# Eight matmuls without a reader, placed in TensorE's stream behind the first part of the last V and ahead of the last group's total, in a two-block decode attention kernel

## The chip, the core and the metric

The kernel runs on one core of one Trainium2 chip. The metric is the device time of one execution in microseconds. The times shown are medians of several executions. Beside them stands one execution that was recorded by the hardware profiler; its span runs from the first to the last instruction, and its own time is a little longer than its span. Engines are called by the profile's names: PE is TensorE's matmul side and PEld its weight loads, DVE is VectorE, ACT is ScalarE, POOL is GpSimd, SP is SyncE, which issues nearly all DMAs.

## The reference

Two independent blocks A and B, of the same shapes, decode one token each with 32 heads of 128 elements over 8192 cached positions. Everything is bf16 in HBM.

```python
q = (x @ wq).reshape(B, Sq, H, Dh).transpose(0, 2, 1, 3)     # x: 1 x 1 x 512, wq: 512 x 4096
scores = einsum("bhqd,bhkd->bhqk", q, k_cache) * Dh ** -0.5  # k_cache: 1 x 32 x 8192 x 128
p = softmax(scores, axis=-1)
o = einsum("bhqk,bhkd->bhqd", p, v_cache)                    # v_cache: 1 x 32 x 8192 x 128
y = o.transpose(0, 2, 1, 3).reshape(B, Sq, H * Dh) @ wo      # wo: 4096 x 512
out = concatenate([y_A, y_B], axis=-1)                       # 1 x 1 x 1024
```

K and V of one block are 64 MiB each, so some 285 MB are read for 2 KB of output.

## The kernel before

**Tiling.** The 64 heads go in 16 rounds of G = 4 heads; rounds 0 to 7 are block A, 8 to 15 block B. In a round a head has 32 partitions and each partition 256 positions (T), so one K or V of a round is a tile of 128 partitions by 256 x 128 elements, 8 MiB. `kn` holds two K tiles, `vn` holds one V tile. At the end `kn` also receives the output weights `wo` of both blocks, in the room of K tiles that are done with.

**One round r.** DVE multiplies K in place by q, in two halves (L280). PE then sums over the 128 elements of a head with matmuls against an identity: `scores` (L425 to L438) runs four tiles, alternately in the two halves of the PSUM tensor `rps`, each with one small matmul that opens the bank (L430) and a loop of four turns with four matmuls of 512 columns each (L432 to L436). DVE reduces each tile to 64 scores per partition (L308). After the fourth tile come the maximum (L313, PE's transpose L476, L315, PE's broadcast L478), ACT's four exponentials into `pt` (L383) and the row sums, which PE adds up over the partitions (L484). Then PE waits for V (L485, semaphore s_v) and multiplies: 64 matmuls of 512 columns into `acc` (L492), which go in turn to four groups of 32 PSUM partitions. The last of them raises c_pv. DVE picks the useful blocks of `acc` in the next round (`part`, L283 to L292), and PE adds them up over the partitions (`total_of_group`, L440 to L442).

**The DMA queue.** SP issues everything in a fixed order: K of round n+2 when the scores of round n are through, V of round n+1 when c_pv says that the V matmuls of round n are done with `vn`. The V of rounds 14 and 15 comes in two DMAs, positions 0 to 191 and 192 to 255 (VT = 192, L207 and L208), on two semaphores. So in these two rounds PE does 48 of the 64 matmuls, enters an `If` and waits for the second part (`w_v2`, L489 and L490), and does the other 16.

**The end.** In round 14 SP also issues `wo` of A (L229) and the first 16 heads of `wo` of B (L230, `load_wob(0)`), then the two parts of the last V when c_pv of round 14 has come (L231), and six smaller pieces of `wo` of B (L233): three of 4 heads, then 2, 1 and 1. In round 15, between the scores and its V, PE runs `mid` (L447 to L467): it lays out the outputs of earlier heads and does the 48 output matmuls of A's 32 and B's first 16 heads (L461). Behind the loop over rounds, PE does the other 16 heads of B piece by piece as the pieces land (L497 to L509, the matmuls at L506, two per head). Ahead of the piece with g = 2 it does `total_of_group` for the last group (L500), which waits for DVE's `part` (c_st). The piece of 2 heads begins with the last group's heads, so it also waits for DVE's normalised output of that group (L297, c_o, waited for at L503). Two copies (L352, L386) and one DMA (L389) end the kernel.

**Order.** The order on each engine is written out by hand, engine by engine; engines meet only at the semaphores named above.

## Time and profile before

| | |
|---|---|
| median of 3 runs | 666.0 us |
| lowest, highest | 665.41, 666.83 us |
| the profiled execution's own time | 665.7 us |
| its span | 664.2 us |
| mean granted clock of TensorE | 0.784 |
| PE, DVE, ACT busy | 385.1 us (58%), 363.3 us (55%), 76.0 us (11%) |
| read from HBM | 285.21 MB, 429 GB/s over the span |

Lines beginning with L are lines of the kernel before. In rows of the timeline the first number is the start in us from the beginning of the span, the second the time from the first start to the last end of the instructions in the row, "x16" their number, and the bracket the idle time of the engine ahead of them with what ended it. "PEclk" is the clock that TensorE was granted, as a share of full speed. The ends of matmuls are modelled by the profiler.

### The profile page before, as it was taken

The numbers are of one execution on the slowest core, as the hardware profiler recorded it, in microseconds if no ns is written. First come the engines' busy times: TensorE is split into PE (matmuls) and PEld (weight loads), VectorE is DVE, ScalarE is ACT, GpSimd is POOL, SyncE is SP. The second block draws the span as 40 slices with busy tenths as digits, with TensorE's granted clock in tenths as the row PEclk, the third lists the DMA queues.
The fourth block names the chain that finished last, engine by engine and source line by source line (L and its number), as shares of the span: only waits on it lengthen the run. The fifth ranks groups of instructions, "written<-read, shape, count | busy, mean of one in ns | idle before, by whom it ended". The sixth has DMA issues, their size and how long they took to land.

```text
span 664.2 us, 7946 instructions
## 1 busy us (share of the span) xinstructions
PE 385.1 (58%) x2398; PEld 169.4 (25%) x2398; DVE 363.3 (55%) x250; ACT 76.0 (11%) x211; POOL 2.3 (0%) x12
## 2 busy tenths in 40 slices
PE   1719392854819275481928548192854819285776
PEld 0203141322304132230413223041322304132332
DVE  1046757548292654829275482927547292754821
ACT  1710202020010202001020200102020010202020
POOL 1000000000000000000000000000000000000000
PEclk9968787786958778695877869597786959778789
DMA  9999999999999999999989999999999999989998
GB/s 379 442 442 442 442 442 391 430 442 442 442 442 399 422 442 442 442 442 442 442 387 434 442 442 442 442 442 414 406 442 442 442 442 442 434 387 458 426 413 344
DMA packets 6472, 285.22 MB, mean 429 GB/s; under 512 B 708, under 2 KB 1224, under 8 KB 1608
## 3 DMA queue, kind: packets, MB, share of 16 engines
q1 hardware_dynamic: 6464, 285.22, 99.5%
q10 hardware_dynamic: 8, 0.00, 0.0%
HBM read 285.21 MB, written 0.00 MB: 429 GB/s over the span
## 4 chain that ended last, share of the span: by engine, by line
DMA 82%; PE 15%; issue 1%; ACT 1%; SPq 0%; ACTq 0%; DVE 0%
DMA vn<-in_A_v_cache_dram 41%; DMA vn<-in_B_v_cache_dram 34%; PE acc L492 13%; DMA kn<-in_B_wo_dram 5%; PE yps L419 2%; DMA vn<-in_A_wq_dram 2%; ACT qmem L372 1%; SPq L220 0%; PE yps L506 0%; SPq L208 0%; ACTq L43 0%; ACTq L372 0%; DVE out_sb L352 0%
## 5 line engine op out<-in xcount | busy, mean ns | idle before, releaser
L280 DVE TENSOR_TENSOR kn<-kn,qmem 128x16384 bf16<-128x16384 bf16 x32 | 276.7, 8688 | 49.6 <-DMA kn<-in_A_k_cache_dram 37.1
L436 PE MATMUL rps<-kn,ident 128*128 x1024 | 236.2, 383 | 0.4
L492 PE MATMUL acc<-vn,pt 128*32 128x512 bf16 x1024 | 92.0, 537 | 153.5 <-DMA vn<-in_A_v_cache_dram 80.4
L308 DVE TENSOR_REDUCE s_sb<-rps 128x64 f32<-128x512 f32 x64 | 44.3, 692 | 166.8 <-PE rps L436 166.8
L436 PEld LDWEIGHTS rps<-kn,ident 128*128 128x128 bf16 x1024 | 96.5, 98 | 110.4 <-issue 22.3
L492 PEld LDWEIGHTS acc<-vn,pt 128*32 128x32 bf16 x1024 | 38.4, 129 | 200.6 <-issue 194.3
L378 ACT ACTIVATE negb<-bmp 128x4 f32<-128x4 f32 x16 | 2.8, 173 | 547.3 <-PE bmp L478 547.3
L383 ACT ACTIVATE pt<-s_sb,negb 32x256 bf16<-32x256 f32 x64 | 54.9, 858 | 4.3 <-ACT negb L378 3.0
L484 PE MATMUL misc<-rsum,ones_f 128*128 128x4 f32 x32 | 9.2, 358 | 56.4 <-ACT pt L383 56.4
L285 DVE TENSOR_SCALAR om<-acc,msk 128x128 f32<-128x128 f32 x16 | 5.6, 350 | 41.8 <-PE acc L492 41.8
L484 PEld LDWEIGHTS misc<-rsum,ones_f 128*128 128x128 f32 x32 | 7.8, 304 | 58.2 <-ACT pt L383 57.7
L419 PE MATMUL yps<-vn,xT 128*128 x64 | 17.4, 422 | 8.5 <-ACT qmem L372 4.4
L288 DVE SCALAR_TENSOR_TENSOR om<-acc,msk,om 128x128 f32<-128x128 f32 x48 | 16.8, 351 | 5.9
L430 PE MATMUL rps<-ones_bf,zrow 1*128 1x1 bf16 x64 | 11.0, 172 | 15.6 <-DVE kn L280 15.4
L476 PE MATMUL mtp<-ident_f,m 128*1 128x128 f32 x32 | 6.1, 270 | 22.6 <-DVE m L313 22.6
L372 ACT CAST qmem<-yps 32x128 f32 x64 | 16.4, 256 | 9.4 <-PE yps L419 8.6
L430 PEld LDWEIGHTS rps<-ones_bf,zrow 1*128 1x128 bf16 x64 | 5.8, 91 | 42.8 <-issue 42.8
L383 ACT ACTIVATION_READ_ACCUMULATOR pt<-s_sb,negb 32x1 f32 x64 | 15.9, 248 | 0.0
L419 PEld LDWEIGHTS yps<-vn,xT 128*128 x64 | 6.6, 103 | 18.9 <-issue 16.0
L478 PE MATMUL bmp<-gm,ones_f 1*128 1x4 f32 x32 | 6.1, 258 | 7.3 <-DVE gm L315 7.3
L297 DVE TENSOR_TENSOR oD<-mtp,rinv 128x4 f32 x15 | 2.4, 162 | 13.6 <-PE mtp L442 13.6
L315 DVE TENSOR_REDUCE gm<-mtp 1x4 f32<-1x128 f32 x16 | 4.5, 279 | 8.9 <-PE mtp L476 8.9
(56 smaller groups left out, 50.9 us busy)
## 6 DMA issues: line engine op xcount, KB each, us to landing
vn<-in_B_v_cache_dram SPq DMA_DIRECT2D x2, 6144.0 KB, 28.0
vn<-in_A_wq_dram SPq DMA_DIRECT2D x1, 4096.0 KB, 12.2
vn<-in_B_wq_dram SPq DMA_DIRECT2D x1, 4096.0 KB, 21.4
vn<-in_B_v_cache_dram SPq DMA_DIRECT2D x2, 2048.0 KB, 32.5
kn<-in_A_wo_dram SPq DMA_DIRECT2D x1, 4096.0 KB, 27.8
kn<-in_B_wo_dram SPq DMA_DIRECT2D x1, 2048.0 KB, 32.3
kn<-in_B_wo_dram SPq DMA_DIRECT2D x3, 512.0 KB, 34.1
kn<-in_B_wo_dram SPq DMA_DIRECT2D x1, 256.0 KB, 35.2
```

Source lines behind the costliest of these rows:

```text
L280: e.tensor_tensor(k, k, qflat[:, bass.ds(q, Dh)].unsqueeze(1).broadcast_to([P, HM, Dh]), ALU.mult).then_inc(c_mul, 2)
L288: e.scalar_tensor_tensor(om[t % 2][:], acc[:, t * Dh:(t + 1) * Dh], msk[:, t:t + 1], om[(t + 1) % 2][:], ALU.mult, ALU.add).then_inc(*((c_ ...
L308: e.tensor_reduce(s_sb[:, h * HT:(h + 1) * HT], rps[:, h % 2, :].rearrange("p (t d) -> p t d", d=DW), AX.X, ALU.add).then_inc(c_sr, 1)
L372: i = e.copy(qflat[p, bass.ds(r * (2 * Dh) + j * Dh, Dh)], yps[j][p, h * Dh:(h + 1) * Dh])
L383: e.activation(pt[p, 0:T, h], s_sb[p, :], AF.Exp, bias=negb[p, h:h + 1], scale=scale, accum_out=rsum[p, h:h + 1]).then_inc(c_p, 4)
L419: i = e.matmul(yps[j][:], xT[:, bass.ds(x0 + c, 1)].broadcast_to([P, P]), vn[:, bass.ds(w0 + (c * H * Dh + j * G * Dh), G * Dh)], start=(c ...
L430: e.matmul(rps[:, tile, 0:1], zrow[:], ones_bf[0:1, 0:1], start=True, stop=False, skip_group_check=True)
L436: m = e.matmul(ro, ident[:], src, start=False, stop=False, skip_group_check=True)
L476: e.matmul(mtp[0:1, 0:P], m1[:], ident_f[:], start=True, stop=True).then_inc(c_gx, 1)
L478: e.matmul(bmp[:, 0:G], ones_f[0:1, :], gm[:], start=True, stop=True).then_inc(c_bc, 1)
L484: e.matmul(misc[:, 0:G], ones_f[:], rsum[:], start=True, stop=True)
L492: m = e.matmul(acc[k:k + HP, :], ptf[:, g * W * G:g * W * G + HP], vn[:, g * W * Dh:(g + 1) * W * Dh], start=(g < G), stop=(g >= NG - G))
```

## The change

A helper `turn_over(n)` is added to PE's stream. It runs n times a loop body of one matmul: the identity as weights, the first 512 columns of `vn` as the moving operand, the first half of `rps` as the target. Each of them starts and stops its own accumulation. Nothing reads the result: in rounds 14 and 15 the scores of the round have been reduced by then, and the next tile of scores opens the bank anew. It waits for no semaphore and raises none.

It is called at two places: with n = 5 inside the `If` for the last two rounds, ahead of `w_v2()`, so in round 14 and in round 15; and with n = 3 behind the loop over rounds, ahead of the last `total_of_group()`. The text holds eight matmuls by this count; one execution runs 5 + 5 + 3 = 13. The instructions of the other engines, and the order of all others on PE, are the same as before.

```diff
+                def turn_over(n):
+
+                    with e.Fori(0, n):
+                        e.matmul(rps[:, 0, :], ident[:], vn[:, 0:512], start=True, stop=True)
+
                 with e.Fori(0, N) as r:
...
                     for g in range(NG):
                         if g * W == VT:
                             with e.If(r >= N - 2):
+                                turn_over(5)
                                 w_v2()
...
                 for g in range(1, len(WOB)):
                     h0, n, rows = WOB[g]
                     if g == 2:
+                        turn_over(3)
                         total_of_group()
```

## The prediction

> **What bounds the kernel now.** I read the page first: the rows of DMA, then the chain that ended last.

> ```profile
> DMA  9999999999999999999989999999999999989998
> GB/s 379 442 442 442 442 442 391 430 442 442 442 442 399 422 442 442 442 442 442 442 387 434 442 442 442 442 442 414 406 442 442 442 442 442 434 387 458 426 413 344
> ...
> DMA 82%; PE 15%; issue 1%; ACT 1%; SPq 0%; ACTq 0%; DVE 0%
> ```

> The 16 DMA engines are busy in all 40 slices, at 442 GB/s in most, and 82% of the chain is DMA. The kernel is bound by reading its caches. PE's 15% stand in the chain because each V is issued when PE's last matmul of the V before has freed `vn`; whether such a piece costs time depends on whether the queue runs dry meanwhile. So next I followed the chain through the last two rounds.

> ```profile
> 618.13 5.96 PE acc L492 x64
> ...
> 626.38 35.17 DMA kn<-in_B_wo_dram
> ...
> 661.59 0.64 PE yps L506 x6
> ...
> 662.28 0.29 PE yps L506 x2
> ...
> 662.59 0.41 DVE out_sb L352
> ```

> The end is set by landings. Piece g = 4 of `wo` lands at 626.38 + 35.17 = 661.55, the last piece at about 662.24, since its two matmuls start at 662.28. Behind that are 0.29 us of PE, 0.41 us of DVE and the output's DMA up to 664.2. The queue at that time, from the timeline of SP and the lists of DMA issues (the number behind KB is the time from issue to landing):

> ```profile
> 605.18 0.43 SPq L220 DMA_DIRECT2D kn<-in_B_wo_dram  x1
> 624.11 0.80 SPq L208 DMA_DIRECT2D vn<-in_B_v_cache_dram  x2
> 624.96 14.94 SPq L220 DMA_DIRECT2D kn<-in_B_wo_dram  x6
> ```

> ```profile
> kn<-in_B_wo_dram SPq DMA_DIRECT2D x1, 2048.0 KB, 32.3
> ```

> ```profile
> vn<-in_B_v_cache_dram SPq DMA_DIRECT2D x1, 6144.0 KB, 27.9
> vn<-in_B_v_cache_dram SPq DMA_DIRECT2D x1, 2048.0 KB, 32.5
> ```

> When the last V is issued at 624.11, the queue still holds work up to 605.18 + 32.3 = 637.5: a reserve of 13.4 us. And the six small pieces, which at 0.43 us each would take under 3 us to issue, take SP 14.94 us, up to 639.90: SP itself is held back by a queue that is full. The last V's parts land at 624.11 + 27.9 = 652.0 and, issued 0.4 us later, near 657.0.

> PE's end, and the two rows of DVE that it exchanges with:

> ```profile
> 652.17 2.77 PE L492 MATMUL acc<-vn,pt 128*32 128x512 bf16 x48
> 657.06 1.05 PE L492 MATMUL acc<-vn,pt 128*32 128x512 bf16 x16 [2.12 <-DMA vn<-in_B_v_cache_dram]
> 658.27 0.60 PE L506 MATMUL yps<-kn,o 128*2 128x256 bf16 x8 [0.16 <-DMA kn<-in_B_wo_dram]
> 659.99 0.38 PE L442 MATMUL mtp<-selh,om 128*128 128x4 f32 x2 [1.12 <-DVE om L288]
> 660.30 1.14 PE L506 MATMUL yps<-kn,o 128*2 128x256 bf16 x16
> 661.59 0.96 PE L506 MATMUL yps<-kn,o 128*2 128x256 bf16 x8 [0.15 <-DMA kn<-in_B_wo_dram]
> ```

> ```profile
> 658.16 0.35 DVE L285 TENSOR_SCALAR om<-acc,msk 128x128 f32<-128x128 f32 x1 [6.95 <-PE acc L492]
> ...
> 660.48 0.17 DVE L297 TENSOR_TENSOR o<-mtp,rinv 128x4 bf16<-128x4 f32 x1 [0.46 <-PE mtp L442]
> ```

> Here are the two waits: 2.12 us ahead of the last 16 matmuls of V and 1.12 us ahead of the total. The last group's output is ready at 660.48 + 0.17 = 660.65, the piece that uses it lands at 661.55: PE's chain has 0.90 us to spare behind the first wait.

> **The change part by part.** Thirteen matmuls are added; nothing is removed. First their price, which no row shows directly. The nearest rows are loops and V matmuls at both clocks:

> ```profile
> 618.51 0.18 PEld L492 LDWEIGHTS acc<-vn,pt 128*32 128x32 bf16 x4 [0.24 <-issue]
> ...
> 622.35 0.18 PEld L492 LDWEIGHTS acc<-vn,pt 128*32 128x32 bf16 x4 [0.24 <-issue]
> ...
> 622.99 0.58 PEld L492 LDWEIGHTS acc<-vn,pt 128*32 128x32 bf16 x16 [0.46 <-issue]
> ...
> 624.11 3.76 PE L436 MATMUL rps<-kn,ident 128*128 x16
> ...
> 636.06 3.73 PE L436 MATMUL rps<-kn,ident 128*128 x16
> ```

> ```profile
> 12.96 0.89 issue
> 13.85 5.11 PE yps L419 x12
> ```

> A row of L436 is the same kind of matmul as the added one (identity, 512 columns, all four row and column groups), with four turns of a loop in it: 3.76 / 16 = 0.235 us each at the full clock. V's matmuls run four side by side: 48 in 2.77 us is 4 x 2.77 / 48 = 0.231 us for one stream of 512 columns at the full clock. The rows from 618.51 to 622.35 are ten groups of four, so a group of four costs (622.35 - 618.51) / 9 = 0.427 us at half clock. The four turns of L436 thus cost at most 3.76 - 16 x 0.231 = 0.06 us beyond the matmuls. Entering a loop costs between nothing and the 0.89 us from the landing of wq to the first matmul of the first loop on PE; I take 0.2, nearer to the low end, because PE has its instructions in hand here and waits for no semaphore. Five matmuls: 5 x 0.235 + 0.2 = **1.4 us**, bounds 5 x 0.231 = 1.2 and, at half clock with the slow entry, 5 x 0.427 + 0.89 = 3.0. Three: 3 x 0.235 + 0.2 = **0.9 us**, bounds 0.7 and 2.2. Nothing below zero is among them, as a matmul gives no time back except through the clock, which is a rival below.

> [...]

> *Round 14, five.* There is no wait to fill here. The weight loads of the last 16 matmuls begin at 622.99, 0.46 us of weight-load idle behind the group before, and the 64 matmuls stand in the chain as one unbroken piece from 618.13. So 1.4 us is pure addition. It delays c_pv, and with it the issue of the last V and the six pieces, from 624.11 to 625.5. The queue's reserve of 13.4 us covers this; without that cover it would cost the 1.4 us in full. The pieces' issue still ends with the full queue, at 639.90. DMA cost: **0**. It also delays all of round 15's scores by 1.4 us, since their tiles follow each other on PE; the fourth then ends near 641.2.

> *From there to the last V* there is the softmax chain and `mid`, and here the clock speaks. The table by windows, cut where the clock steps:

> ```profile
> 639.76:643.17 3.41, 1.10 (x7) 0.67 (x6) 1.58 (x5) 0.45 (x2) 0.00 (x0) 1.00 1.07 461
> 643.17:646.59 3.42, 2.53 (x18) 0.99 (x22) 1.74 (x10) 3.17 (x8) 0.00 (x0) 0.50 1.06 460
> 646.59:650.00 3.41, 3.41 (x36) 1.11 (x32) 0.00 (x0) 0.00 (x0) 0.00 (x0) 0.50 1.07 461
> 650.00:653.41 3.41, 2.61 (x38) 1.14 (x34) 0.69 (x1) 0.00 (x0) 0.00 (x0) 1.00 0.72 308
> 653.41:656.83 3.42, 1.53 (x31) 0.60 (x20) 0.00 (x0) 0.00 (x0) 0.00 (x0) 1.00 0.91 382
> 656.83:660.24 3.41, 1.90 (x26) 0.90 (x26) 1.49 (x5) 0.00 (x0) 0.00 (x0) 1.00 1.01 401
> ```

> The columns are the window, its length, the busy time of PE, PEld, DVE, ACT and POOL, PEclk, the DMA share and GB/s. The steps fall on a grid of 3.41 us. A window with 1.10 us of PE is followed by half clock, one with 1.53 us is not; a full one is followed by full clock, one with 2.53 us is not. On the same grid the change brings 1.4 us more of scores into the first of these windows and pushes 0.8 us of the softmax's matmuls out: 1.7 us, above 1.53, so `mid` runs at full clock. Its 48 matmuls of four side by side took

> ```profile
> 645.47 4.98 PE L461 MATMUL yps<-kn,o 128*2 128x512 bf16 x48
> ```

> and would take 48 x 0.231 / 4 = 2.8: 2.2 us back against the 1.4 lost. Then PE waits for the first part of V at 652.0 and begins its 48 as before. On another position of the grid, with `mid` as slow as before, the 1.4 us arrive whole: the 48 begin at 653.6.

> *Round 15, five.* The 48 end at 654.9, or at 656.3 in the bad case; with 1.4 us more, 656.3 or 657.7. The second part lands at 657.0: cost **0**, or 0.7 us, which the 0.90 us to spare behind it take up. If the fillers were dearer, what is late next is the last group's output.

> *The three.* They start behind the eight matmuls at 658.27 + 0.60 = 658.9 and end at 659.8, ahead of the total at 659.99: cost **0**. At their upper bound they would end at 661.1 and the total would be 1.1 late, 0.2 past the spare.

> SBUF and PSUM: the fillers read `vn` while DMA writes `kn` and `vn`, as the scores and V's matmuls do all along; slices of 442 GB/s stand over busy and idle PE alike, so I count nothing, in either direction. The sum is 0 + 0 + 0 against the profiled execution: 665.7 us, its span 664.2 and 1.5 around it. It lies 0.3 under the median of 666.0. I put the forecast at **665.8**, between the two, since the profiled execution had no half clock in its end and a slower run may have.

> **The rivals.** A measurement of this kernel can tell about 0.2%, 1.3 us, from no change.

> *Slower: PE becomes the bound at the end.* The mechanism is the delay of round 14 carried through round 15 and added to the five there. Cover is 2.12 us of wait and 0.90 us behind it, 3.0 in all; the forecast's demand in the bad case is 1.4 + 1.4 = 2.8. From 1.5 us for five matmuls on, the end moves, by twice what lies above that. For: the margin is thin, and entry is a guess. With the slow entry at full clock five cost 5 x 0.235 + 0.89 = 2.1: 4.2 - 3.0 = 1.2 late, 667.0. At half clock throughout, 6.0 - 3.0 = 3.0, 668.8. Against: `mid` runs nearly unbroken for 5 us, which brings the clock back, and the clock may return more than is lost.

> *Faster: the clock in the end.* The two waits are where a window could fall under 1.53 us of PE. Then the last 16 of V cost 16 x 0.427 / 4 = 1.7 instead of 1.05, and the 24 small ones behind the total up to double their pace; with the landing times fixed that makes some 0.5 to 1.4 us. The fillers add 1.2 and 0.7 us of PE to these windows and forbid it. For: the spread of the three runs, 665.41 to 666.83, is of that size, and the grid need not lie the same in each run. Against: the table above shows PEclk 1.00 from 650.00 on, so there is nothing to gain in it, and what stands behind the last landing at full clock is not shortened. Gone from a slow run: 666.8 - 1.4 = 665.4, still within 0.2% of 666.0.

> [...]

> *The change doesn't do what it says:* that the fillers miss the waits is true for five of the thirteen, as worked out; 666.0 as well, by the reserve.

> **How the numbers follow.** No difference, in any of its forms: 0.86 (forecast 0.66, clock regained in part of the runs 0.14, rule or missed waits 0.06). Slower by PE: 0.10 over 1.3 us; its milder form, up to 667.0, is inside "same". Faster by over 1.3 us needs less than 664.7, 0.7 under the lowest run, and would need landings that come earlier: 0.04. The range goes from 665.1, somewhat under the lowest run, to 667.1, the slow entry at full clock.

> **What would show it.** Right: the chain again ends in the small pieces of `wo`, landing within 0.3 us of 661.55 and 662.24; SP's issue at 625.3 to 625.7 and ending near 640; the five in 1.2 to 1.7 us; a wait left ahead of the last 16 of V, or under 0.9 us of delay. Wrong: L506's last matmuls released by DVE's output instead of a landing; fillers at over 0.4 us each; a queue that is empty after 637.

## The result, and the profile after

| | before | after |
|---|---|---|
| median of 7 runs each | 666.1 us | 668.71 us |
| lowest, highest | 665.41, 666.83 us | 666.41, 669.14 us |
| ratio of after to before | | 1.0037, 95% interval 1.0027 to 1.0047 |
| the profiled execution's own time | 665.7 us | 669.1 us |
| its span | 664.2 us | 664.0 us |
| its time outside the span | 1.5 us | 5.1 us |
| instructions in PE's built program | 478 | 492 |

The change makes the kernel slower by 0.37%, and yet the span did not get longer. All seven executions of the changed kernel have spans of 663.9 to 664.1 us. What grew is the part of an execution that lies outside the span: 4.3 to 5.1 us in six of them and 2.3 in the seventh. Ahead of the span the profiles show no growth: the first packet of instructions is recorded 11.1 us ahead of the first instruction before, and 11.2 after. Of the kernel before, 68 more executions were taken beside the experiments below; one of them, of 797.38 us, was in a slower state and is left out of all counts and ratios.

Inside the span everything stands as it did. The chain through the last two rounds, of the changed kernel (start, length, what):

```profile
622.94 1.19 PE rps L472 x5
624.13 1.01 PE acc L498 x16
625.13 0.02 issue
625.15 0.33 SPq L208
...
627.42 33.97 DMA kn<-in_B_wo_dram
661.39 0.04 issue
661.43 0.62 PE yps L513 x6
...
662.08 0.29 PE yps L513 x2
662.37 0.02 issue
662.40 0.41 DVE out_sb L352
```

The five fillers of round 14 (L472) take 1.19 us of the chain. The chain then goes through the same pieces of `wo`, which land at 661.39 and near 662.05, no later than before. PE's fillers and the waits that they stand in, from the timeline of PE:

```profile
652.29 2.77 PE L498 MATMUL acc<-vn,pt 128*32 128x512 bf16 x48
655.00 1.25 PE L472 MATMUL rps<-vn,ident 128*128 128x512 bf16 x5
656.90 1.05 PE L498 MATMUL acc<-vn,pt 128*32 128x512 bf16 x16 [0.65 <-DMA vn<-in_B_v_cache_dram]
658.65 0.82 PE L472 MATMUL rps<-vn,ident 128*128 128x512 bf16 x3
```

and the total behind the three, from the timeline of all engines:

```profile
659.83 0.38 PE L442 MATMUL mtp<-selh,om 128*128 128x4 f32 x2 [0.36 <-DVE om L288]
```

The five of round 15 fit the first wait and leave 0.65 us of it; the three fit the second and leave 0.36. So where did the 2.6 us of the medians go? The list of DMA queues, taken for the time behind the span, points to an answer. From 664 us on, of the kernel before (queue, packets, MB, share):

```profile
q14 instruction: 1, 0.01, 0.1%
```

and of the changed kernel, in the stretch from 666 to 668 us:

```profile
q8 instruction: 1, 0.02, 4.3%
```

A second kind of instruction packet appears there, on queue q8, of 16384 bytes. It starts 2.0 us behind the last instruction's end and takes 1.4 us. The instructions added are the 14 in PE's program, and four more in every other engine's: the two loops consist of four blocks, and each engine's program ends in one entry for every block. So the other engines do the same work as before, but their programs are not quite the same.

### The profile page after: what moved, and what is told of

The parts are those of the page before. It is cut to its first block, busy times and chain, and to the rows that moved or that the text cites. A ratio compares the mean times of both kernels' runs of the same rounds, so it can differ in the third digit from the quotient of the medians.

```text
span 664.0 us, 8001 instructions
## 1 busy us (share of the span) xinstructions
PE 386.3 (58%) x2411; PEld 169.5 (26%) x2411; DVE 363.2 (55%) x250; ACT 76.0 (11%) x211; POOL 2.3 (0%) x12
## 4 chain that ended last, share of the span: by engine, by line
DMA 82%; PE 15%; issue 1%; ACT 1%; SPq 0%; ACTq 0%; DVE 0%
DMA vn<-in_A_v_cache_dram 41%; DMA vn<-in_B_v_cache_dram 34%; PE acc L498 13%; DMA kn<-in_B_wo_dram 5%; DMA vn<-in_A_wq_dram 2%; PE yps L419 2%; ACT qmem L372 1%; SPq L220 0%; PE rps L472 0%; PE yps L513 0%; SPq L208 0%; ACTq L372 0%; ACTq L43 0%; DVE out_sb L352 0%
## 5 line engine op out<-in xcount | busy, mean ns | idle before, releaser
L436 PE MATMUL rps<-kn,ident 128*128 x1024 | 236.2, 383 | 0.4
L436 PEld LDWEIGHTS rps<-kn,ident 128*128 128x128 bf16 x1024 | 96.5, 98 | 110.6 <-issue 25.2
L285 DVE TENSOR_SCALAR om<-acc,msk 128x128 f32<-128x128 f32 x16 | 5.6, 350 | 41.1 <-PE acc L498 41.1
L419 PE MATMUL yps<-vn,xT 128*128 x64 | 17.3, 418 | 8.6 <-DMA vn<-in_A_wq_dram 4.4
L288 DVE SCALAR_TENSOR_TENSOR om<-acc,msk,om 128x128 f32<-128x128 f32 x48 | 16.8, 351 | 5.9
L419 PEld LDWEIGHTS yps<-vn,xT 128*128 x64 | 6.6, 103 | 18.9 <-issue 16.1
L297 DVE TENSOR_TENSOR oD<-mtp,rinv 128x4 f32 x15 | 2.4, 161 | 13.6 <-PE mtp L442 13.6
## 6 DMA issues: line engine op xcount, KB each, us to landing
vn<-in_B_v_cache_dram SPq DMA_DIRECT2D x2, 6144.0 KB, 27.4
vn<-in_B_v_cache_dram SPq DMA_DIRECT2D x2, 2048.0 KB, 31.9
kn<-in_B_wo_dram SPq DMA_DIRECT2D x1, 2048.0 KB, 32.3
```

Of the source, the lines that this page charges most:

```text
L288: e.scalar_tensor_tensor(om[t % 2][:], acc[:, t * Dh:(t + 1) * Dh], msk[:, t:t + 1], om[(t + 1) % 2][:], ALU.mult, ALU.add).then_inc(*((c_ ...
L419: i = e.matmul(yps[j][:], xT[:, bass.ds(x0 + c, 1)].broadcast_to([P, P]), vn[:, bass.ds(w0 + (c * H * Dh + j * G * Dh), G * Dh)], start=(c ...
L436: m = e.matmul(ro, ident[:], src, start=False, stop=False, skip_group_check=True)
```

## The experiments

Three theories stood against each other. The **length** theory: PE's program passes an edge at which one more page of it, a packet of 16384 bytes like the one on q8, has to be fetched. The **block** theory: the entries at the end of each engine's program cost the time. The **run** (later filler) theory: the matmuls run near the end make what follows longer. In the expectations, an instruction count is that of the built program. The table has all twelve runs; "outside" is an execution's own time less its span, and the last column is where the profiled execution shows the q8 packet.

| | what | PE's program | span, us | outside, us | median, us | ratio to before, 95% interval | q8 packet |
|---|---|---|---|---|---|---|---|
| e11 | all fillers, score tiles share code | 471 | 663.9 to 665.4 | 1.4 to 1.8 | 666.38 | 1.0005, 0.9996 to 1.0014 | none |
| e7 | all fillers, one matmul a turn in the scores | 474 | 806.1 to 808.2 | 1.4 to 1.5 | 808.56 | 1.214, 1.2125 to 1.2156 | inside, near the end |
| e4 | all fillers, q projection in one bank | 480 | 681.5 to 682.0 | 1.5 to 2.4 | 683.7 | 1.0261, 1.0247 to 1.0275 | behind |
| e3 | no fillers, two loops on POOL | 482 | 663.9 to 664.9 | 1.4 to 2.5 | 665.68 | 0.9998, 0.9988 to 1.0007 | behind |
| e8 | the fives alone | 485 | 663.9 to 664.4 | 1.4 to 1.6 | 665.52 | 0.9994, 0.9985 to 1.0003 | none |
| e9 | the three alone | 485 | 664.0 to 664.4 | 1.4 to 3.2 | 665.6 | 1.0001, 0.9992 to 1.0010 | behind |
| e10 | no fillers, 5 tiny matmuls | 488 | 664.0 to 664.9 | 4.9 to 5.3, one 2.1 | 669.14 | 1.0043, 1.0027 to 1.0059 | behind |
| e6 | no fillers, 6 tiny matmuls | 490 | 664.0 to 665.1 | 4.8 to 5.1 | 669.6 | 1.0054, 1.0041 to 1.0067 | behind |
| e5 | the changed kernel again | 492 | 663.9 to 664.1 | 4.8 to 5.4, one 2.4 | 668.93 | 1.0039, 1.0025 to 1.0054 | behind |
| e1 | all fillers, no loops | 494 | 665.0 to 665.3 | 1.4 to 2.5 | 666.78 | 1.0014, 1.0005 to 1.0023 | inside, at 75 us |
| e2 | no fillers, 8 tiny matmuls | 494 | 665.1 to 666.4 | 1.4 to 1.8 | 667.25 | 1.0019, 1.0010 to 1.0028 | inside, at 75 us |
| e12 | no fillers, 10 tiny matmuls | 498 | 665.1 to 666.6 | 1.4 to 2.5 | 667.32 | 1.0027, 1.0015 to 1.0039 | inside, at 75 us |

The kernel before, at 478, was run 67 times beside these: 55 executions have 1.4 to 1.8 us outside the span and 12 have 2.0 to 2.8.

### e1, the fillers without loops

```diff
 def turn_over(n):
-    with e.Fori(0, n):
+    for _ in range(n):
         e.matmul(rps[:, 0, :], ident[:], vn[:, 0:512], start=True, stop=True)
```

> The same 13 fillers, written out one after the other instead of in two loops. PE's program has 494 instructions (before 478, after 492); the other engines' programs are as before, because no loop is added (the change gave each of them 4 more, one for each block of a loop). Length theory (the time outside the span jumps when PE's program passes some length between 478 and 492): as slow as the change, 668.3 to 669.1 us with a span near 664.0. Block theory (the 4 extra block entries at the end of every engine's program cost it): 665.5 to 666.8. Run theory (fillers executed near the end cost it): 668.3 to 669.1.

No theory had this. The time outside fell back to 1.4 to 2.5 us, but the span grew to 665.0 to 665.3. The growth is early. The first V's row in the chain of the kernel before, and the same row of e1:

```profile
35.61 45.11 DMA vn<-in_A_v_cache_dram
```

```profile
35.94 46.28 DMA vn<-in_A_v_cache_dram
```

The first V lands 1.2 us later after its issue, and everything behind it is shifted by that. In that stretch, from 75 to 76.5 us, e1's DMA queues have

```profile
q8 instruction: 1, 0.02, 4.4%
```

a packet as at the changed kernel's end, now in round 0. The run theory falls with it: the 13 fillers ran, and nothing was slow behind them.

### e2, length without fillers

```diff
+for c in range(8):
+    e.matmul(rps[:, 0, 0:NA], xrow[:, c % C:D:C], ident[0:NA, 0:NA], start=True, stop=True)
 e.wait_ge(s_w[0], 16)
```

> No fillers at all. Instead PE has eight tiny matmuls (2 columns) near the kernel's start, while it waits for the first weights: PE's program has 494 instructions, the other engines' are as before. Length theory: 668.3 to 669.1 us with a span near 664.1. Block theory and run theory: 665.5 to 666.8.

The kernel has no filler and no new block, and is slow in the same way as e1: q8 at 75 us, the first V 46.60 us after its issue instead of 45.11. Its median is 0.5 us above e1's. Both kernels have 494 instructions. The effect is of the length; that at 494 it stands in the span and at 492 behind it was not foreseen.

### e3, blocks without fillers

```diff
-e.memset(zrow[:], 0.0).then_inc(c_pool, 1)
-e.memset(rsum[:], 0.0).then_inc(c_pool, 1)
+with e.Fori(0, 1):
+    e.memset(zrow[:], 0.0).then_inc(c_pool, 1)
+with e.Fori(0, 1):
+    e.memset(rsum[:], 0.0).then_inc(c_pool, 1)
```

> No fillers. Two of POOL's first memsets get a loop of one turn each. That adds four block entries to every other engine (PE 482 instructions, SP 95, ACT 103, DVE 141, as in the change) and ten instructions to POOL (72). Length theory: fast, 665.5 to 666.8 us, if the length that matters is above 482. Block theory: 668.3 to 669.1. Run theory: 665.5 to 666.8.

665.68 us, the same as before: the block entries cost nothing that can be measured. The block theory falls.

### e4, the changed kernel with a shorter q projection

```diff
-with e.Fori(0, N // 2) as r:
+with e.Fori(0, N) as r:
...
-    for j in range(2):
+    for j in range(1):
         e.wait_ge(c_qa, by_tile)
```

The offsets into the weights, ACT's copies and the counts that are waited for follow this and are not shown.

> The changed kernel with its fillers in loops, but PE's loop over the q projection has one PSUM bank in turn instead of two written out, which takes 12 instructions from PE's program: 480, while the other engines keep the extra block entries. The q projection gets some us longer, behind the K loads that are in the queue anyway, so the span should stay within 0.5 of 664.0. Length theory: 665.3 to 666.8 us. Block theory and run theory: 668.3 to 669.1.

The time outside the span is 1.5 to 2.4 us with all fillers and all block entries in place, which speaks for the length alone. The span is a miss: with one PSUM bank, PE waits for ACT's copy in each of the 16 steps but the first, and a step takes 3.47 us (rows of e4's timeline of PE):

```profile
14.12 1.88 PE L419 MATMUL yps<-vn,xT 128*128 x4 [4.75 <-DMA vn<-in_A_wq_dram]
17.60 1.89 PE L419 MATMUL yps<-vn,xT 128*128 x4 [1.59 <-ACT qmem L372]
...
66.23 1.89 PE L419 MATMUL yps<-vn,xT 128*128 x4 [1.59 <-ACT qmem L372]
```

The first V is issued at 68.15 instead of 35.61, and by then the K loads that were to hide it are through.

### e5 and e6, the changed kernel again and 490 without fillers

After e1 to e4 the length theory had its sharper form, the page theory: one more packet of 16384 bytes is fetched, in round 0 or behind the last instruction, as the length of PE's program has it. The expectation of e5 calls it the third; that is the author's count, which no run shows. e5 is the changed kernel word for word. e6 has the edit of e2 with 6 in place of 8.

> The changed kernel once more, on the chip of the runs beside it (PE's program 492 instructions). Page theory (a third 16 KB page of PE's program has to be fetched: behind the last instruction when only what follows the kernel lies in it, during round 0 when the kernel itself reaches it): span 664.0, a q8 instruction packet of 16384 bytes behind the span, 2.3 to 5.1 us outside the span, 667 to 669 us in all. Filler theory (the fillers at run time make what follows longer): the same numbers. Chip theory (the first measurement was made on another chip, whose ends are longer): 1.5 us outside the span, 665.5.

> No fillers; six tiny matmuls near the start of PE's stream bring its program to 490 instructions. Page theory: span 664.0 to 664.3, no instruction packet inside the span, one of 16384 bytes on q8 behind it, 2.3 to 5.1 us outside, 667 to 669 us. Filler theory and chip theory: 1.5 us outside the span, 665.5.

e5 repeats the first measurement beside a kernel before on the same chip, so it is not the chip. e6 is the decisive run: a kernel with no filler, no added loop and six matmuls of two columns 650 us ahead of the end is slow by 0.54%, with 4.8 to 5.1 us outside its span. From 664 us on its queues show

```profile
q8 instruction: 1, 0.02, 0.3%
```

The filler theory and the chip theory fall; the page theory holds in that the length of PE's program decides.

### e7, all fillers in 474 instructions

```diff
-NI = 4
+NI = 1
```

> The changed kernel with both fillers, but the loop over the scores' matmuls has one matmul in its body instead of four (16 turns instead of 4), which brings PE's program to 474 instructions. The scores get some 0.1 to 0.3 us a tile longer, behind the DMA. Page theory: span 664.0 to 664.3, no q8 packet, 1.5 us outside, 665.5. Filler theory: 2.3 to 5.1 us outside, 667 to 669.

Outside the span 1.4 to 1.5 us, as the page theory has it. But in the profiled execution the q8 packet, which the theory did not expect at 474, is there: it starts 0.69 us ahead of the last instruction's end, and no cost shows. The span is again a miss. One matmul in a turn, with its address worked out in a register, takes half a microsecond:

```profile
305.26 1.86 PE L436 MATMUL rps<-kn,ident 128*128 x4 [0.15 <-issue]
307.27 1.86 PE L436 MATMUL rps<-kn,ident 128*128 x4 [0.15 <-issue]
```

that is (307.27 - 305.26) / 4 = 0.50 us a turn, at PEclk 1.00, against 0.235 a matmul with four in a turn. PE becomes the bound, at 70% busy.

### e8 and e9, one half of the change at a time

e8 leaves out `turn_over(3)`, e9 leaves out `turn_over(5)`.

> The five fillers of rounds 14 and 15 alone, without the three: PE's program has 485 instructions. Page theory: the q8 packet again behind the span, with fewer instructions beyond the page's edge than at 492; 1.5 to 3.5 us outside, 665.5 to 667.5 us. Filler theory: the three near the end are gone, so 1.5 us outside, 665.5.

> The three fillers ahead of the last total alone, without the fives: PE's program has 485 instructions, as with the fives alone, which were fast. Page theory: 1.45 us outside the span, 665.3 to 666.0 us. Filler theory (the three, run 4 us before the end, make what follows longer): 4 to 5 us outside, 668 to 669.

e8 by itself came out as the filler theory had it: 1.4 to 1.6 us outside and none of the packet that the page theory expected. e9, with the three fillers near the end and as fast, goes against the filler theory. Each half alone is the same as before within 0.1%, and together they cost 0.37%. What they add up is the length: 478 + 7 = 485 twice, 478 + 14 = 492 together. In e9's profiled execution the packet comes behind the span and 2.9 us lie outside; most of its others have 1.4 to 1.6.

### e10, where the edge is

The edit of e2 with 5 in place of 8.

> No fillers; five tiny matmuls near the start bring PE's program to 488 instructions, between 485 (fast) and 490 (slow). Page theory: either 1.45 us outside the span or 4.3 to 5.4, nothing between in most executions, and the instruction packet behind the span with the slow one; it places the edge. Filler theory: 1.45 us.

488 instructions, no fillers: 4.9 to 5.3 us outside in five executions, 2.1 in one. With e8 and e9 the edge lies above 485 and at or below 488.

### e11, all fillers in 471 instructions

```diff
-ro = rps[:, tile, :].rearrange("p (t d) -> p t d", d=DW)
-e.matmul(rps[:, tile, 0:1], zrow[:], ones_bf[0:1, 0:1], start=True, stop=False,
+at = e.snap(tile * 512, min_val=0, max_val=512)
+rf = rps[:].rearrange("p a b -> p (a b)")
+ro = rf[:, bass.ds(at, 512)].rearrange("p (t d) -> p t d", d=DW)
+e.matmul(rf[:, bass.ds(at, 1)], zrow[:], ones_bf[0:1, 0:1], start=True, stop=False,
...
-with e.Fori(0, NB // 2):
-    for tile in range(2):
-        scores(tile)
-        e.reg_add(koff, koff, HT * Dh - Dh)
+with e.Fori(0, NB) as t:
+    scores(t % 2)
+    e.reg_add(koff, koff, HT * Dh - Dh)
```

> The changed kernel with all 13 fillers, but the two score tiles of a turn share one piece of code whose PSUM half is picked by a register, so PE's program has 471 instructions. Page theory: 1.45 us outside the span, and if the scores keep their 3.7 us a tile, a span of 663.8 to 664.3 and 665.2 to 665.8 us: the fillers as such cost nothing. Filler theory: 4 to 5 us outside the span whatever the span is.

With the 13 fillers run at the same places, 1.4 to 1.8 us lie outside and no q8 packet is recorded. The span (663.9 to 665.4) was expected at 663.8 to 664.3: each tile now has 0.37 us of idle PE ahead of it,

```profile
629.92 0.17 PE L432 MATMUL rps<-ones_bf,zrow 1*128 1x1 bf16 x1 [0.37 <-issue]
630.15 3.73 PE L438 MATMUL rps<-kn,ident 128*128 x16
634.24 0.17 PE L432 MATMUL rps<-ones_bf,zrow 1*128 1x1 bf16 x1 [0.37 <-issue]
634.46 3.73 PE L438 MATMUL rps<-kn,ident 128*128 x16
```

and in its profiled execution the chain's last part runs over PE. It gives back what the shorter program saves; no kernel here is clearly faster than the one before.

### e12, longer still

The edit of e2 with 10 in place of 8.

> No fillers; ten tiny matmuls bring PE's program to 498 instructions. Page theory: as with 494, the instruction packet inside the span in round 0, 1.0 to 2.0 us more span (665.1 to 666.1), 1.45 us outside, 666.5 to 667.6 us; so longer is then cheaper than 490. Filler theory: 665.5.

As at 494: the packet at 75 us, the first V 46.50 us after its issue, 1.4 to 2.5 us outside, 667.32 us. The spans reach 666.6, where up to 666.1 was expected. So 498 instructions are cheaper than 488 to 492.

## Why the prediction was wrong

**The step that failed** is the sum's last one: "The sum is 0 + 0 + 0 against the profiled execution: 665.7 us, its span 664.2 and 1.5 around it". The three zeros hold. The 1.5 was carried over as if no edit could touch it, and it became 5.1 in the profiled execution and 4.3 to 5.4 in 11 of the 13 executions of the changed kernel. The prediction priced thirteen matmuls by their running time and gave no price to the 14 instructions of program that they are. At 478 the program ended 8 to 10 instructions short of an edge, and no row of the profile before says so; the count of the built program would have, to someone who knows that an edge exists. The signs of being right that the prediction named lie inside the span, and they came true there, but for the last V's issue, 0.15 us earlier than the earliest it named; none of them could show this loss.

The trace gives the size of what is fetched: one packet of 16384 bytes. The runs give its price: 3.4 us behind the span at 488 to 492, and 1.2 to 1.8 us of the medians at 494 and 498. How many instructions such a packet holds is not shown, and of the edge only that it lies between 485 and 488.

**Point by point.** *DMA, and the delay of round 14:* right. SP issued the last V at 625.15, 1.0 us later than before, and the pieces of `wo` landed no later. SP's issue of the six pieces again ended with the full queue:

```profile
626.00 13.77 SPq L220 DMA_DIRECT2D kn<-in_B_wo_dram  x6
```

at 639.77, against the "near 640" of the forecast.

*Five and three fillers:* right within 0.2 us. Five cost 1.19 us where 1.4 was taken, three 0.82 where 0.9 was. A loop's entry costs next to nothing here: five matmuls at 0.235 make 1.18 us, three 0.71.

*`mid` at full clock:* wrong. The forecast read from one row that over 1.53 us of PE in a window keeps the clock. The changed kernel's table by windows, cut at its own steps:

```profile
639.54:642.95 3.41, 1.61 (x8) 0.47 (x6) 1.37 (x3) 0.00 (x0) 0.00 (x0) 1.00 1.07 461
642.95:646.36 3.41, 2.01 (x14) 1.26 (x18) 1.94 (x12) 2.60 (x7) 0.00 (x0) 1.00 1.07 461
646.36:649.77 3.41, 3.41 (x36) 1.19 (x32) 0.00 (x0) 1.03 (x4) 0.00 (x0) 0.50 1.07 461
```

The window of 1.61 us kept it, the next one, of 2.01 us, lost it. So busy time alone is not what decides. The 48 matmuls took 4.45 us where 4.98 was before and 2.8 was forecast: 0.5 us came back instead of 2.2. It cost nothing, because the five fillers behind it still ended 0.65 us ahead of the second part of V.

*The slower rival:* right in sign, wrong in its cause. PE did not become the bound in the end; 0.65 us of the first wait were left. That its figure for half clock throughout, 668.8, lies beside the measured 668.71 is luck.

*The clock in the end:* the mechanism is there, and it is small. The kernel before has spans of 664.4 us or more in 16 of its 67 executions beside the experiments, up to 665.6; the changed kernel's 13 executions all lie between 663.9 and 664.1. A kernel without fillers shows what a longer span is. The table by windows of e6's profiled execution, span 664.7:

```profile
656.00:658.00 2.00, 1.05 (x17) 0.39 (x18) 0.12 (x1) 0.00 (x0) 0.00 (x0) 1.00 1.04 418
658.00:660.00 2.00, 1.29 (x10) 0.64 (x10) 1.38 (x5) 0.00 (x0) 0.00 (x0) 0.51 1.01 393
660.00:662.00 2.00, 2.00 (x20) 1.32 (x22) 0.17 (x1) 0.00 (x0) 0.00 (x0) 0.50 0.65 209
```

PEclk falls to 0.50 at 658, and the eight matmuls of `wo` that start there take 1.01 us instead of the 0.60 of the kernel before, the total 0.59 instead of 0.38. No idle piece of PE near that step is over 2.12 us. The profiles of e2 and e12, without fillers too, also show 0.50 in the end, from 659.6 on and from 653.2 to 656.6; the changed kernel's profiles keep 1.00 from 649.8 to the end. On the average of the spans (664.26 for the 67, 664.01 for the 13) that is worth 0.25 us at most, a tenth of the 2.6 us by which the median rose; no run separates the clock's part of it.

*"The change doesn't do what it says":* as forecast, the five of round 14 have no wait to fill; the other eight stand in the two waits of the end.

**What stays open.** That the length of PE's program decides is shown: without fillers and padded to 488 or 490 the kernel is slow, and at 485 each half of the change is free. No trace shows what waits for the page behind the last instruction; that it is waited for is argued from the time, not seen. In the fourteen profiled executions the two go together without exception: where the packet comes behind the span, 2.3 to 5.1 us lie outside; where it starts within it or is not recorded, 1.4 to 1.8.

The traces give one more hint. In e3, e4 and e9, at 480 to 485 instructions, the packet ends 2.86, 2.62 and 3.25 us behind the last instruction, and 2.55, 2.32 and 2.94 us lie outside the span, 0.3 less each time, as if the execution ended with the packet. In the changed kernel, e5, e6 and e10 it ends at 3.43, 3.01, 2.73 and 3.32, and 5.06, 4.77, 4.95 and 4.94 lie outside, 1.6 to 2.2 more. So at 488 to 492 something follows the packet that takes about as long as what lies outside the span in a kernel without it (1.4 to 1.8). That would fit an end that lies in the fetched page and can't start before it has come, which is argued from seven executions and not tested.

It is not settled why the page is fetched in round 0 at 494 and more and only behind the end at 488 to 492, nor why a kernel of 478, 482 or 485 instructions has 2.0 to 3.2 us outside in a few executions; in a profile the packet was seen at 474, 480, 482 and 485, and not at 478.

## What to carry to other kernels

Compare an execution's own time with its span before looking for a loss inside the span; if the difference moved, list the DMA queues behind the last instruction. Count the instructions of each engine's built program when an edit adds code, even code that fills idle time, and test an edit's length apart from its work by padding the kernel before to the same count. Two halves that are free alone (here 665.52 and 665.6 us) and slow together (668.71) point to such an edge.
